# One weight load moved from ScalarE's DMA queue to GpSimd's, in front of the identity

## The chip, the cores and the metric

The kernel runs on one core of a Trainium2 chip. The metric is the device time of one execution in microseconds (us), as a median over runs. The engines are named as in the profile: PE is TensorE (matmul), PEld its weight loads, DVE VectorE, ACT ScalarE, POOL GpSimd, SP SyncE; SPq, ACTq and POOLq are the queues of instructions that these issue, DMA issues among them.

## The reference

One input x of 2048 rows and 512 columns goes through two branches that a gate mixes:

```
g = sigmoid(sum(x * gate_w, last axis))
a = attention(x): q, k, v = x @ wqkv, 32 heads of 16; row s sees the rows s, s-2, ..., s-14;
    softmax over these 8 (bfloat16), weighted sum of v, then @ wo
b = mixer(x): h = layernorm(x); u = gelu(h^T w1 + b1); y = (u w2 + b2)^T
out = g * a + (1 - g) * b
```

All inputs and the output are bfloat16. wqkv is 512 x 1536, wo 512 x 512, w1 2048 x 1792, w2 1792 x 2048.

## The kernel before, in words

The kernel is one list of operations that a planner in the same file (class `_Sched`) puts into an order for each engine. Each operation carries a duration, the buffers it reads and writes (these give waits on semaphores) and further order constraints: `order` holds operations that must be issued earlier by the plan, without a wait on their end. For the first loads the time at which they land is written by hand (`lands`). The planner walks through the operations by their ready times and the length of the work that hangs on them; then each engine runs its list in order, and no engine passes a waiting instruction of its own.

The 512 columns of x are the contraction of the projections, taken as four parts of 128 (`dt` 0 to 3). So wqkv's columns for q, k and v are each loaded as rows of 128 by part: "Wq's first quarter" is the first 128 rows of the 512 columns for q, 128 KB, one row of 1 KB for each partition. The projections need x transposed (`XT`), 512 rows of x at a time (a block `sb`, 0 to 3).

How the program begins:

- SP issues the DMA transpose of x's first 512 rows, columns 128 to 511 (line 473), then Wq's second, third and fourth quarter (one DMA each), Wk in two halves, two tiles of x, the DMA transpose of the second block (line 460), and further loads.
- ACT issues "the plain columns" (line 479): columns 0 to 127 of the first 512 rows, not transposed, 128 KB; and behind it Wq's first quarter (line 481, through `ld_w`, whose DMA appears as line 429 like that of all plain DMAs).
- POOL writes the identity (line 417), 128 x 128, and clears the padding columns of K and V (lines 420, 421) and the bias row buffer (line 517).
- PE runs five matmuls over 512 columns and one over 256 on a constant (line 536), whose result nobody reads; then four matmuls of the plain columns against the identity (line 544), which transpose them; and another constant matmul. ACT (line 553) and DVE (line 555) each evict half of the transposed columns into XT's first part. DVE's first operation is a reduction of the identity to a 0/1 matrix (line 424) that is used later for summing over heads.
- Then come PE's projections (line 617). For the first block, eight results (four column groups of q, four of k) are summed in eight PSUM banks at once: four matmuls for q's column groups with part 0, four with part 1, four with part 2, four with part 3; then k's with parts 0 and 1, and with parts 2 and 3. So the first four matmuls need Wq's first quarter and the transposed plain columns, the next four Wq's second quarter and the DMA transpose, and so on. The rest of the projections (other blocks, then v) sum four matmuls each in four banks in turn, and ACT evicts them (lines 625, 628).

What comes after: DVE multiplies q with shifted k (line 688), PE sums the products over each head (line 696, two bursts), DVE and ACT do the softmax, ACT's DMAs spread the weights over partitions, DVE forms the weighted sums of v (lines 795 to 800). Beside it DVE takes the layernorm's statistics (line 572), ACT applies it (line 596), and PE runs the mixer's two matmuls (lines 810 and 860). At the end PE multiplies by wo (line 876) and DVE adds the gated branches (line 897), and the rows go out by DMA. The order on DVE and ACT is largely written out by hand in chains of names; PE's main matmuls are in one chain with the product sums placed by the planner.

The issue order around the change is set by these lines: `first_loads` gives Wq's first quarter its queue, and one line orders it behind the plain columns.

Of the kernel before, what the change touches and what calls it, by code (L numbers as in the profile page):

```python
# [333 lines left out]
def bass_gated_mix__sliding_local_dilated__mixer_token_mlp__prompt_kernel(nc, A_x, A_wqkv, A_wo, B_x, B_w1, B_b1, B_w2, B_b2, gate_w, out, dbg=None):  # L334
    with contextlib.ExitStack() as es:
# [75 lines left out]
        def psub(ap_, p0, np_, offs, dims):  # L411
# [5 lines left out]
        c_ident = A("pool", lambda e: e.affine_select(out=IDENT, in_=nc.const_aps.tensor(1.0, [128, 128], BF16), pattern=[[1, 128]], compare_op=ALU.is_equal,  # L417
                                                     fill=0.0, base=0, channel_multiplier=-1),
                    0.4, writes=["ident"], name="ident")
# [8 lines left out]
        def mk_dma(dst, src):  # L428
            return lambda e: e.dma_start(dst, src)  # L429
# [3 lines left out]
        def throttle():  # L433
            return [init_dmas[-5]] if len(init_dmas) >= 5 else []

        def prev_dma():
            return [init_dmas[-1]] if init_dmas else []

        def ld_x(t0, n, q="sp"):
            ds = sch.dsem("x%d" % t0)  # L440
            op = sch.dma(q, mk_dma(X[:, t0:t0 + n, :], xv[:, t0:t0 + n, :]), n * 128 * D * 2, ds,
                         writes=["x%d" % t for t in range(t0, t0 + n)], deps=throttle() if q == "sp" else [], after=prev_dma() if q == "sp" else [], name="d_x%d" % t0)
            if q == "sp":
                init_dmas.append(op)
            return op

        def ld_w(tn, d0, n, q="sp"):
            ds = sch.dsem("wqkv%d_%d" % (tn, d0))
            op = sch.dma(q, mk_dma(WQKV[:, d0:d0 + n, tn * D:(tn + 1) * D], wqkv_v[:, d0:d0 + n, tn * D:(tn + 1) * D]),
                         n * 128 * D * 2, ds, writes=["wqkv%d_%d" % (tn, dt) for dt in range(d0, d0 + n)],  # L450
                         deps=throttle() if q == "sp" and n == 4 else [], after=prev_dma() if q == "sp" else [],
                         issue=0.65 if n == 4 else 0.45, name="d_wp%d_%d" % (tn, d0))
            if q == "sp":
                init_dmas.append(op)
            return op
# [14 lines left out]
        def ld_xt0():  # L470
            ds = sch.dsem("xt0")
            dst = XT[:, 1:4, 0:512]
            op = sch.dma("sp", lambda e: e.dma_start_transpose(dst, x2d[0:512, 128:512]), 512 * 384 * 2, ds, issue=1.25,
                         writes=XT0[1:4], after=prev_dma(), name="d_xt0")
            init_dmas.append(op)
            return op

        XP = view("OUTS", BF16, [(128, 4), (1, 128)])
        d_xp = sch.dma("act", mk_dma(XP, xv[:, 0:4, 0:128]), 512 * 128 * 2, sch.dsem("xp"), writes=["outs0"], issue=0.4, name="d_xp")

        first_loads = [ld_w(0, 0, 1, "act"), ld_xt0(), ld_w(0, 1, 1), ld_w(0, 2, 1), ld_w(0, 3, 1), ld_w(1, 0, 2), ld_w(1, 2, 2),
                       ld_x(0, 2)]
        ld_xt(1)
        first_loads.append(init_dmas[-1])
# [1 line left out]
            op_.lands = t_  # L486
            op_.deps.clear()
        d_xp.lands = 3.1
        first_loads[0].order.add(d_xp)
        init_dmas[:] = [first_loads[1]] + first_loads[5:]  # L490
        ld_x(2, 2)
        ld_x(4, 4)
# [558 lines left out]
```

## Time and profile before

| | us |
|---|---|
| median of 3 runs | 167.71 (167.71 to 167.93) |
| the profiled execution | 168.55 |
| its span, first to last instruction | 167.3 |
| PE busy | 162.1 |
| DVE busy | 151.3 |
| ACT busy | 75.1 |
| POOL busy | 0.7 |
| plain columns: issued by ACT, length of the issue | 0.80, 0.46 |
| Wq's first quarter: issued by ACT, length of the issue | 1.28, 0.53 |
| identity on POOL: start, length | 0.89, 0.29 |
| first projection matmul | 5.61 |

The profile is one execution; its times count from its first instruction. The issue of a DMA is an instruction on the issuing engine's queue; the data arrive later, and the DMA view of the trace gives the time from the issue's start to the landing. Matmuls overlap their neighbours, so their start distances tell their rate better than their durations. The mean clock that the profile grants PE over the span is 1.000.

### The profile page before, as it was taken

Reading aid. Unit: us, or ns where it says so; the run is one execution under the profiler, and the core shown is the slowest. Engines: PE = TensorE matmul, PEld = TensorE weight load, DVE = VectorE, ACT = ScalarE, POOL = GpSimd, SP = SyncE. Lnnn points to the kernel's source line nnn. Section 1 sums busy time; section 2 is a strip of 40 time slices with the busy share of each in tenths; the row PEclk is TensorE's granted clock in tenths of the full one; section 3 lists DMA queues with packets and bytes.
Section 4 is the critical chain, followed back from the end, with each engine's and each line's share of the span. In section 5 each row is a group of like instructions: output and inputs, shape, how many; then the busy total and the mean of one; then the engine's idle time right before and its main releaser. Section 6 shows DMA issues by size and latency. Waiting matters only on the chain.

```text
span 167.3 us, 2136 instructions
## 1 busy us (share of the span) xinstructions
PE 162.1 (97%) x845; PEld 77.5 (46%) x859; DVE 151.3 (90%) x154; ACT 75.1 (45%) x116; POOL 0.7 (0%) x8
## 2 busy tenths in 40 slices
PE   7699999999999999999999999999999999999994
PEld 2355555554454444444444444444444444444463
DVE  1055999999999999999999999999999999999896
ACT  3077688889899818793131121131231321310100
POOL 1000000000000000000000000000000000000000
PEclk9999999999999999999999999999999999999999
DMA  5999999959003846996779926462672570000454
GB/s 135 327 268 216 314 316 290 303 165 308 2 0 97 311 116 179 307 290 155 181 189 340 339 76 142 113 187 71 181 218 83 138 223 0 0 0 0 157 190 159
DMA packets 47625, 29.64 MB, mean 177 GB/s; under 512 B 9856, under 2 KB 46464, under 8 KB 47616
## 3 DMA queue, kind: packets, MB, share of 16 engines
q1 hardware_dynamic: 45120, 24.85, 54.4%
q10 hardware_dynamic: 2496, 4.66, 10.2%
q8 instruction: 7, 0.11, 0.3%
q14 instruction: 2, 0.02, 0.0%
HBM read 21.24 MB, written 2.10 MB: 140 GB/s over the span
## 4 chain that ended last, share of the span: by engine, by line
PE 91%; DMA 3%; DVE 2%; ACT 2%; issue 1%; ACTq 0%
PE ps L860 29%; PE ps L810 29%; PE ps L617 23%; PE ps L876 6%; PE ps L696 4%; DMA arena<-in_A_wqkv_dram 3%; DVE arena L897 2%; ACT L585 1%; ACT arena L628 1%; ACTq L429 0%; ACT arena L585 0%
## 5 line engine op out<-in xcount | busy, mean ns | idle before, releaser
L860 PE MATMUL ps<-arena 128*128 128x512 bf16 x220 | 48.5, 379 | 0.2
L810 PE MATMUL ps<-arena 128*128 128x512 bf16 x219 | 48.2, 379 | 0.4 <-issue 0.2
L617 PE MATMUL ps<-arena 128*128 128x512 bf16 x188 | 41.4, 379 | 1.6 <-DMA arena<-in_A_wqkv_dram 1.3
L688 DVE TENSOR_TENSOR arena<-arena 128x4096 bf16<-128x4096 bf16 (+1 forms) x12 | 35.5, 2998 | 2.5 <-ACT arena L628 2.1
L795 DVE TENSOR_TENSOR arena<-arena 128x8192 bf16<-128x8192 bf16 x8 | 35.0, 4419 | 0.0
L860 PEld LDWEIGHTS ps<-arena 128*128 128x128 bf16 x224 | 21.9, 98 | 26.4
L810 PEld LDWEIGHTS ps<-arena 128*128 128x128 bf16 x224 | 21.8, 98 | 26.6 <-ACT arena L726 0.4
L617 PEld LDWEIGHTS ps<-arena 128*128 128x128 bf16 x192 | 21.6, 113 | 21.5 <-issue 1.8
L928 ACT ACTIVATE arena<-ps,arena 128x512 bf16<-128x512 f32 x16 | 12.5, 778 | 39.4 <-PE ps L860 39.4
L798 DVE TENSOR_TENSOR arena<-arena 128x4096 bf16<-128x4096 bf16 (+1 forms) x16 | 27.0, 1751 | 0.0
L628 ACT ACTIVATE arena<-ps 128x512 bf16<-128x512 f32 x32 | 18.6, 596 | 4.5 <-PE ps L617 4.5
L831 ACT ACTIVATE arena<-ps,arena 128x512 bf16<-128x512 f32 x14 | 9.6, 687 | 22.2 <-PE ps L810 16.6
L572 DVE BATCH_NORM_STATS2 arena<-arena 128x6 f32<-128x512 bf16 x16 | 10.0, 682 | 6.1 <-DMA arena<-in_A_x_dram 6.1
L876 PE MATMUL ps<-arena 128*128 128x512 bf16 (+1 forms) x79 | 14.1, 336 | 0.1
L897 DVE SCALAR_TENSOR_TENSOR arena<-ps,arena 128x512 bf16<-128x512 f32 (+1 forms) x20 | 11.5, 637 | 0.9 <-PE ps L876 0.7
L596 ACT ACTIVATE arena<-arena 128x512 bf16<-128x512 bf16 x16 | 12.2, 804 | 0.0
L625 ACT ACTIVATE arena<-ps 128x512 bf16<-128x512 f32 x16 | 9.0, 597 | 6.2 <-PE ps L617 6.1
L876 PEld LDWEIGHTS ps<-arena 128*128 128x128 bf16 x80 | 7.8, 98 | 6.2
L672 DVE SCALAR_TENSOR_TENSOR arena<-arena 128x512 bf16<-128x512 bf16 x16 | 10.1, 689 | 0.0
L742 DVE TENSOR_TENSOR arena<-arena 128x512 bf16<-128x512 bf16 (+4 forms) x11 | 7.3, 667 | 0.6 <-ACT arena L761 0.2
L696 PE MATMUL ps<-arena 128*32 128x512 bf16 x128 | 7.3, 380 | 0.0
L726 ACT ACTIVATE arena<-ps 128x512 bf16<-128x512 f32 x8 | 4.7, 592 | 4.6 <-PE ps L696 4.6
(42 smaller groups left out, 40.0 us busy)
## 6 DMA issues: line engine op xcount, KB each, us to landing
arena<-in_B_w_dram SPq DMA_DIRECT2D x7, 1024.0 KB, 8.5
arena<-in_B_w_dram SPq DMA_DIRECT2D x8, 896.0 KB, 5.2
arena<-arena ACTq DMA_DIRECT2D x32, 128.0 KB, 2.9
arena<-in_A_x_dram SPq DMA_DIRECT2D x4, 512.0 KB, 6.1
out_dram<-arena SPq DMA_DIRECT2D x14, 128.0 KB, 1.7
arena<-in_A_x_dram SPq DMA_DIRECT2D x1, 1536.0 KB, 7.9
arena<-in_A_wqkv_dram SPq DMA_DIRECT2D x2, 256.0 KB, 3.8
arena<-in_A_x_dram SPq DMA_DIRECT2D x2, 256.0 KB, 3.6
```

Source lines behind the costliest of these rows:

```text
L596: A("act", (lambda t_: (lambda e: e.activation(out=X[:, t_, :], in_=X[:, t_, :], func=AF.Identity, scale=col(RSTD, t_), bias=col(NMR, t_)) ...
L617: ins = e.matmul(ps[:, bank, s0:s1], lhsT=lhsT, rhs=XT[:, dt, sb * 512 + s0:sb * 512 + s1], start=(dt == 0 and s0 == 0), stop=(dt == 3))
L628: return lambda e: e.activation(out=dst, in_=ps[:, bank, :], func=AF.Copy)
L688: return lambda e: e.tensor_tensor(out=PBL[buf][:, :, 512 * c0:512 * (c0 + nc_)], in0=in0, in1=in1, op=ALU.mult)
L696: ins = e.matmul(ps[32 * c:32 * c + 32, 4 + wl, :], lhsT=RP, rhs=PBL[buf][:, wl, c * 512:(c + 1) * 512], start=(dl == 0), stop=(dl == 3), ...
L795: A("dve", (lambda o_, i0, i1: (lambda e: e.tensor_tensor(out=o_, in0=i0, in1=i1, op=ALU.mult)))(pv, in0, in1), 4.4, reads=v_res + ["atx_% ...
L798: A("dve", (lambda pv_, n__: (lambda e: e.tensor_tensor(out=pv_[:, 0:n__], in0=pv_[:, 0:n__], in1=pv_[:, n__:2 * n__], op=ALU.add)))(pv, n ...
L810: ins = e.matmul(ps[:, bank, :], lhsT=W1W[:, slot, st, 128 * e_:128 * e_ + 128], rhs=X[:, st, :], start=(st == 0), stop=(st == NST - 1))
L860: ins = e.matmul(ps[:, bank, :], lhsT=W2S[slot][:, ft, 128 * e_:128 * e_ + 128], rhs=UT[:, ft, :], start=(ft == 0), stop=(ft == NFT - 1))
L876: ins = e.matmul(ps[:, bank, 0:c1 - c0], lhsT=OT[:, t, 128 * i:128 * i + 128], rhs=WO[:, t, c0:c1], start=(t == 0), stop=(t == 3))
L897: A("dve", (lambda i_, b_, c0_, c1_: (lambda e: e.scalar_tensor_tensor(out=T1[:, i_, c0_:c1_], in0=ps[:, b_, 0:c1_ - c0_], scalar=col(G, i ...
L928: A("act", (lambda i_, bank_: (lambda e: e.activation(out=T1[:, i_, :], in_=ps[:, bank_, :], func=AF.Identity, scale=col(OMG, i_), bias=co ...
```

## The change

Wq's first quarter is issued by POOL instead of ACT. The order constraint that put it behind the plain columns on ACT is gone; in its place the identity is ordered behind this issue on POOL. Size, source and destination of the transfer, the hand-written landing times and everything else stay as they are.

```
-        first_loads = [ld_w(0, 0, 1, "act"), ld_xt0(), ld_w(0, 1, 1), ld_w(0, 2, 1), ld_w(0, 3, 1), ld_w(1, 0, 2), ld_w(1, 2, 2),
+        first_loads = [ld_w(0, 0, 1, "pool"), ld_xt0(), ld_w(0, 1, 1), ld_w(0, 2, 1), ld_w(0, 3, 1), ld_w(1, 0, 2), ld_w(1, 2, 2),
...
-        first_loads[0].order.add(d_xp)
+        c_ident.order.add(first_loads[0])
```

## The prediction

> **What bounds the kernel now.** I read the page's shares of busy time and the chain that ended last first. They say which engine sets the end.
>
> ```profile
> span 167.3 us, 2136 instructions
> ...
> PE 162.1 (97%) x845; PEld 77.5 (46%) x859; DVE 151.3 (90%) x154; ACT 75.1 (45%) x116; POOL 0.7 (0%) x8
> ...
> PE 91%; DMA 3%; DVE 2%; ACT 2%; issue 1%; ACTq 0%
> ```
>
> TensorE (PE) is busy for 97% and holds 91% of the chain. The 3% of DMA is one piece. The same chain in order of time, cut to its first 14 us, shows it (start, length, what):
>
> ```profile
> 0.80 0.46 ACTq L429
> 1.25 0.03 issue
> 1.28 4.24 DMA arena<-in_A_wqkv_dram
> 5.52 0.09 issue
> 5.61 8.36 PE ps L617 x38
> ```
>
> ACT issues the plain columns of x from 0.80, then Wq's first quarter from 1.28. The quarter lands 4.24 us later, at 5.52, and the first projection matmul starts at 5.61. From there the chain is PE with pieces of ACT, down to a DVE tail. So the change touches the one transfer that sets PE's start. How much earlier PE may go is set by what else the first matmuls need. The timeline of the same stretch (start, length, engine, line) gives it:
>
> ```profile
> 0.80 1.35 SPq L473 DMA_TRANSPOSE arena<-in_A_x_dram  x1
> 0.84 2.51 PE L536 MATMUL ps<-const-bfloat16-1.0 128*128 128x512 bf16 x6 [0.84 <-PEq L1036]
> 0.89 0.29 POOL L417 TENSOR_SCALAR_AFFINE_SELECT arena<-const-bfloat16-1.0 128x128 bf16<-128x128 bf16 x1 [0.38 <-POOLq L1036]
> 3.33 0.58 PE L544 MATMUL ps<-arena 128*128 128x128 bf16 x4
> 3.71 0.63 PE L536 MATMUL ps<-const-bfloat16-1.0 128*128 128x512 bf16 x1
> 3.96 0.42 DVE L555 CAST arena<-ps 128x256 bf16<-128x256 f32 x1 [2.45 <-PE ps L544]
> ```
>
> The identity is ready at 1.18, the plain columns at 3.2, the PE transposes start at 3.33 and their second half is evicted by 4.38. So on the x side the first matmul could start near 4.43. The second group of four matmuls needs the DMA transpose and Wq's second quarter. The DMA issues that fall into 2.00 to 2.25 (size, us from the start of the issue to the landing) name both:
>
> ```profile
> arena<-in_A_wqkv_dram SPq DMA_DIRECT2D x1, 128.0 KB, 3.8
> arena<-in_A_x_dram SPq DMA_TRANSPOSE x1, 4.9
> ```
>
> The transpose, issued at 0.80, lands at 5.7. The second quarter is issued at 2.22 (SP's timeline) and lands at 2.22 + 3.8 = 6.02. That is the next wall, only half a microsecond behind the one removed.
>
> **The change, part by part.** *The quarter's issue leaves ACT.* ACT loses one issue of 0.53 us (1.28 to 1.81). ACT's table load moves up behind it. ACT's first work is the eviction at 3.74, which waits for PE: nothing gained there. The plain columns are still ACT's first issue at 0.80. SP's queue is not touched.
>
> *The quarter's issue on GpSimd (POOL).* It can start where the identity did, near 0.8. That is 0.48 earlier than 1.28. The trace of before holds no DMA that POOL issues, so both its issue time and its start are bounded by rows. The plain columns were issued at 0.80 and their queue moved 62 packets before 2.25, with none before 2.0: a start of 1.3 us. Wq's quarter was issued at 1.28, and its queue stood like this in 3.25 to 3.5:
>
> ```profile
> q1 hardware_dynamic: 272, 0.07, 122.4%
> q10 hardware_dynamic: 4, 0.00, 4.6%
> ```
>
> None of its packets ran from 3.0 to 3.25, four here: a start of 2.1 us, with the SP queue (q1) full of the transpose. From there, 3.4, to the landing at 5.52 is 2.1 us. On POOL: 0.8 + 1.3 + 2.1 = 4.2 at best, 0.8 + 2.1 + 2.1 = 5.0 with the late start. I take 4.5, nearer the first: like the plain columns it finds the DMA engines empty (no traffic before 2.0 in the DMA view). The farthest row, the slowest landing of a load in the first 14 us (a DMA transpose, 6.0), would give 6.8.
>
> *What waits behind it on POOL.* Identity, two K/V pad memsets and the bias-row memset come after the issue. An issue on ACT or SP takes 0.42 to 0.56 for plain copies here, 1.35 for the first transpose, 3.4 for a later one. The identity, 0.29, is wanted at 3.3 with the plain columns; with an issue of 0.5 it ends at 1.6, with 1.35 at 2.5. Both are hidden by the 2.1 us between 1.18 and 3.3. If it took 3.4, the identity would end at 4.5, and the eviction, 1.05 behind the transposes' start, at 5.65: slower by some 0.1. The DVE reduction over the identity goes with it and is wanted at 38.5, its engine next at 3.96. The K pad is wanted at 11.4, the bias rows at 31.4.
>
> *The shared DMA engines.* The quarter's 128 KB now run beside the plain columns instead of in the middle of the transpose. From 3 to 4 us the engines move 305 GB/s, so 128 KB cost 0.43 us of all of them. At worst the plain columns land that much later, 3.63. The evictions then end at 4.81 and the first group starts at 4.86. At best they're untouched: 4.43. I take 4.8. The transpose and the second quarter have the same bytes ahead of them as before, so I leave 5.7 and 6.02; the bounds are 0.43 earlier (the quarter runs before 2.25, when the engines still have room) and 0.1 later.
>
> *The sum.* Matmuls start 0.215 apart (5.61, 5.83, 6.04), so a group of four takes 0.86. Before: 5.61 + 0.86 = 6.47 for the second group, and its data (6.02) are there. After: the first group runs 4.8 to 5.66, the second waits for the second quarter: 6.02 + 0.09 = 6.11. Gain 6.47 - 6.11 = 0.36 us, wherever the first quarter lands before 5.16. The third and fourth quarters (issued at 2.83 and 3.29, 3.4 and 3.3 to landing) are there at 6.2 and 6.6, wanted at 6.97 and 7.83. The next x block is there at 5.27 + 5.5 = 10.8, wanted at 12.2. No further wall.
>
> *Does it reach the end?* DVE, 90% busy, could eat it. It starts its long run at 15.07 after a wait for evictions of PE's output, and near the end it waits for PE again:
>
> ```profile
> 15.07 2.29 DVE L688 TENSOR_TENSOR arena<-arena 128x4096 bf16<-128x4096 bf16 x1 [2.06 <-ACT arena L628]
> ...
> 157.35 8.29 DVE L897 SCALAR_TENSOR_TENSOR arena<-ps,arena 128x512 bf16<-128x512 f32 x15 [0.72 <-PE ps L876]
> ```
>
> Both move with PE. DVE's last load-bound work ahead of 15.07 ends at 13.02, so that wait has 2 us of room. PE's bursts over DVE's products begin at 38.5 and 61.2, 1.2 us after DVE finished them. The whole program slides by 0.36. The profiled execution took 168.55 us (span 167.3 and 1.25 around it), giving 168.19. The median of the three runs shown is 167.71, 0.84 below it; there I predict 167.35, 0.21% less. A difference under 0.2%, 0.34 us, can't be told from no change, so the forecast lies just on the faster side.
>
> **The rivals.**
> *Only the issue's lead, or less (same).* If POOL's DMA starts later than any row shows, 3.2 to 3.7 us after its issue would still land it at about 5.2 to 5.8, and the second wall stops mattering: time changes by less than 0.2%. For it: nothing in the trace shows POOL's path. Against: it needs a start over 1 us worse than the late row. [...]
>
> *POOL's DMA is late (slower).* Place: PE's wait at 5.61. It decides when the landing is behind 5.52, and shows beyond 5.86. Each microsecond behind it is a microsecond of the end: at 6.1 the time is 168.3, at the far row's 6.8 it is 169.0. For it: no row of such a DMA. Against: three rows put it at 4.2 to 5.0.
>
> *PE is still slow when it starts (slower).* The first matmuls over 512 columns average 624 ns, those from 5.61 on 379. The warm ones' weight loads stand 0.43 apart (1.22, 1.65, 2.08), the later matmuls 0.215. The change to full speed fell between 3.71, the start of the last slow one, and 5.61, with PE busy almost without a gap from 0.84 to 4.34. A plain-column landing at 3.63 opens a gap of 0.4 at 3.3. If that delayed full speed by another such stretch (3.5 us, from 0.84 to 4.34), to 7.8 or later, matmuls from 6.11 to 7.8 would run at half speed: 0.85 lost, net +0.5, 168.2, and more if later. If the change only keeps its moment, nothing is lost: half-speed matmuls from 4.86 are through with the group by 6.11 even if it falls at 5.61. [...]
>
> *More is gained (faster).* If the quarter is through early enough that the second quarter lands up to 0.43 earlier, the gain is up to 0.79: 166.92.
>
> That another order on POOL keeps the issue from being first is cheap: its memsets take 0.15 each, three of them 0.45, still under 5.16.
>
> **How the numbers follow.** The forecast's case 52%: its own range 167.15 to 167.55, by the second quarter's landing between 5.8 and 6.2; of it 44% faster by over 0.2%, 8% within. Only the lead: 9%, within. Late on POOL: 24%, of it 3% within and 21% slower; a price with no row of its own gets more than its rows would give. Slow PE: 9%, slower. More gained: 6%, faster. Sum: faster 0.50, same 0.20, slower 0.30. The range runs from 166.95, the bound of more gain, to 168.4, a landing at 6.2; left out are late landings beyond it (10%), most of the slow PE (7%) and 2% below.
>
> **What would show it.** Right: POOL's first entry is the DMA issue near 0.8, the identity ends before 3.3, the quarter lands before 5.16, the first group starts at 4.4 to 4.9, and a short wait of PE for the second quarter or the transpose ends near 6.1; the wait at 15.07 and the tail come 0.36 earlier. Wrong: PE's first wait still ends on the first quarter; the identity or the eviction at 4.38 moves beyond 5.1; matmuls of L617 average above 379 ns; or PE stands idle later on a DVE or DMA wait that before did not have.

## The result, and the profile after

The changed kernel took 170.27 us (median of four executions, 168.5 to 170.72), the kernel before 167.82 beside it (four, 167.71 to 168.03): an estimated ratio of 1.0113, with a 95% interval of 1.0075 to 1.0152. A second comparison (twelve executions of the changed kernel, 35 of the one before) gave 1.0077, interval 1.0030 to 1.0123. All ratios here leave out executions over 1.5% above the fastest of their kernel, which takes out 7 of those 35 and none of the twelve; over all of them the means are 169.83 and 168.74, a ratio of 1.0065. The change makes the kernel slower; 167.35 had been forecast.

One thing about these times has to be known before they can be read: the executions of *both* kernels lie in two groups about 2 us apart, with nothing between 169.0 and 169.7. Of 16 executions of the changed kernel, 4 lie at 168.3 to 168.5 and 12 at 169.9 to 170.7. Of 100 executions of the kernel before, timed beside the changed kernel and beside the runs below or repeated in them, 71 lie at 167.6 to 169.0 and 29 at 169.8 to 170.9. The executions shown ahead of the prediction, and those beside the first result, happened to be of the lower group.

The profiled execution of the changed kernel took 170.23. The page's lines for the span, the engines and the projections:

```profile
span 169.0 us, 2136 instructions
...
PE 163.9 (97%) x845; PEld 77.9 (46%) x859; DVE 151.3 (90%) x154; ACT 75.1 (44%) x116; POOL 1.5 (1%) x9
...
L617 PE MATMUL ps<-arena 128*128 128x512 bf16 x188 | 43.3, 391 | 1.5 <-DMA arena<-in_A_wqkv_dram 1.1
```

PE is 1.8 us busier with the same 845 matmul records, and the projections (line 617) average 391 ns instead of 379. So the time isn't in a wait: PE itself was slower. The chain of the first 14 us (start, length, what; x31 counts the matmuls that fall into these 14 us):

```profile
0.70 0.59 issue
1.29 4.08 DMA arena<-in_A_wqkv_dram
5.37 0.09 issue
5.46 8.71 PE ps L617 x31
```

The first projection starts 0.15 *earlier* than in the trace of before (5.61), and yet 31 matmuls now take longer (8.71) than 38 did (8.36). The weight loads of the same stretch show where (start, length; one load precedes each matmul):

```profile
5.43 0.14 PEld L617 LDWEIGHTS ps<-arena 128*128 128x128 bf16 x2 [1.69 <-issue]
5.84 0.15 PEld L617 LDWEIGHTS ps<-arena 128*128 128x128 bf16 x1 [0.27 <-issue]
6.27 0.15 PEld L617 LDWEIGHTS ps<-arena 128*128 128x128 bf16 x1 [0.28 <-issue]
...
8.83 0.15 PEld L617 LDWEIGHTS ps<-arena 128*128 128x128 bf16 x1 [0.28 <-issue]
9.26 4.65 PEld L617 LDWEIGHTS ps<-arena 128*128 128x128 bf16 x22 [0.28 <-issue]
```

Up to 9.26 the loads stand 0.43 apart, the pace of the constant matmuls at the start ("half pace" below); from there 22 of them take 4.65, 0.21 each ("full pace"). Nine matmuls at 0.21 extra are 1.9 us. Everything behind is only shifted: DVE's wait for the first evictions and its last wait for PE both end 1.71 later (15.07 and 157.35 before), as the span is 1.7 longer:

```profile
16.78 4.49 DVE L688 TENSOR_TENSOR arena<-arena 128x4096 bf16<-128x4096 bf16 x2 [2.33 <-ACT arena L628]
...
159.06 8.29 DVE L897 SCALAR_TENSOR_TENSOR arena<-ps,arena 128x512 bf16<-128x512 f32 x15 [0.72 <-PE ps L876]
```

And GpSimd's side, from the timeline of the start:

```profile
1.29 0.69 POOL L429 DMA_DIRECT2D arena<-in_A_wqkv_dram  x1 [0.78 <-POOLq L1036]
2.08 0.31 POOL L417 TENSOR_SCALAR_AFFINE_SELECT arena<-const-bfloat16-1.0 128x128 bf16<-128x128 bf16 x1
...
3.31 0.58 PE L544 MATMUL ps<-arena 128*128 128x128 bf16 x4
3.69 0.63 PE L536 MATMUL ps<-const-bfloat16-1.0 128*128 128x512 bf16 x1
```

The issue shows at 1.29, not near 0.8, and takes 0.69; the identity is ready at 2.39, well ahead of PE's transposes, which start when they did. PE is busy from 0.84 to 4.32, as before, and then has nothing to do until the quarter is there.

### The profile page after: what moved, and what is told of

Same layout as the page of the kernel before. It is cut to its first block, busy times and chain, and to the rows that moved or that the text cites. A ratio compares the mean times of both kernels' runs of the same rounds, so it can differ in the third digit from the quotient of the medians.

```text
span 169.0 us, 2136 instructions
## 1 busy us (share of the span) xinstructions
PE 163.9 (97%) x845; PEld 77.9 (46%) x859; DVE 151.3 (90%) x154; ACT 75.1 (44%) x116; POOL 1.5 (1%) x9
## 3 DMA queue, kind: packets, MB, share of 16 engines
q10 hardware_dynamic: 2352, 4.52, 9.9%
## 4 chain that ended last, share of the span: by engine, by line
PE 91%; DMA 2%; DVE 2%; ACT 2%; issue 1%; POOLq 0%
PE ps L860 28%; PE ps L810 28%; PE ps L617 24%; PE ps L876 6%; PE ps L696 4%; DMA arena<-in_A_wqkv_dram 2%; DVE arena L897 2%; ACT L585 1%; ACT arena L628 1%; ACT arena L585 0%; POOLq L1036 0%
## 5 line engine op out<-in xcount | busy, mean ns | idle before, releaser
L860 PE MATMUL ps<-arena 128*128 128x512 bf16 x220 | 48.5, 379 | 0.2
L810 PE MATMUL ps<-arena 128*128 128x512 bf16 x219 | 48.2, 379 | 0.4 <-issue 0.2
L617 PE MATMUL ps<-arena 128*128 128x512 bf16 x188 | 43.3, 391 | 1.5 <-DMA arena<-in_A_wqkv_dram 1.1
```

Source lines behind the costliest of these rows:

```text
L617: ins = e.matmul(ps[:, bank, s0:s1], lhsT=lhsT, rhs=XT[:, dt, sb * 512 + s0:sb * 512 + s1], start=(dt == 0 and s0 == 0), stop=(dt == 3))
L810: ins = e.matmul(ps[:, bank, :], lhsT=W1W[:, slot, st, 128 * e_:128 * e_ + 128], rhs=X[:, st, :], start=(st == 0), stop=(st == NST - 1))
L860: ins = e.matmul(ps[:, bank, :], lhsT=W2S[slot][:, ft, 128 * e_:128 * e_ + 128], rhs=UT[:, ft, :], start=(ft == 0), stop=(ft == NFT - 1))
```

## The experiments

The theory that came out of the traces, not yet shown here: PE starts at half its pace (weight loads 0.43 apart) and goes over to full pace (0.21) at a moment that is not fixed in the program; it lies ahead of 5.61 in the trace of before and at 9.26 in that of the changed kernel. If PE goes on working, this costs little. If it pauses for a microsecond behind its 3.5 us of constant matmuls (1.13 in the changed kernel's trace), the pause can push that moment to 9 or 10 us, and 7 to 11 projections run at half pace. The rivals: GpSimd's DMA, or its traffic, holds PE down; the order on GpSimd does it; the upper group is chance that has nothing to do with the first loads.

### Both kernels again, a GpSimd DMA elsewhere, and a filled pause

The first two are the kernels unchanged; then

```
late_pool (on the kernel before):
-        sch.dma("sp", mk_dma(GWB, gsrc), ...
+        sch.dma("pool", mk_dma(GWB, gsrc), ...
after_fill (on the changed kernel; four constant matmuls behind the transposes, not one):
-    w3_ = A("pe", f_warm(1), 0.43, ...
+    w3_ = A("pe", f_warm(4), 0.43, ...
```

> The kernel before once more, for a second trace of it. In the first trace PE reached full speed before its first projection matmul (5.61), and Wq's first quarter landed at 5.52. [...]

> The changed kernel once more. Its trace had nine projection matmuls 0.43 apart from 5.46 on, where the kernel before has them 0.215 apart: 9 x 0.21 = 1.9 us. [...]

> The kernel before, with a GpSimd DMA elsewhere: the broadcast of gate_w (128 KB, issued near 51 us) goes out from GpSimd instead of SP, the start is as in before. [...]

> The changed kernel with four constant matmuls instead of one behind the transposes, so that PE is busy from 0.84 to its first projection instead of stopping at 4.3. [...] Rival (the GpSimd DMA or its traffic keeps PE slow): still nine slow matmuls up to 9.3, 170.2.

| | executions | of them above 169.6 | median below 169.6 |
|---|---|---|---|
| kernel before, beside them | 35 | 10 | 168.07 |
| before, repeated | 10 | 1 | 167.94 |
| changed, repeated | 12 | 9 | 168.34 |
| GpSimd DMA at 51 us | 10 | 2 | 168.41 |
| changed, pause filled | 12 | 0 | 168.45 |

The fill removes the upper group from the changed kernel (0 of 12 against 9 of 12), with the same DMA on GpSimd: neither that DMA nor its traffic by itself holds PE down. A GpSimd DMA somewhere else doesn't raise the share (2 of 10). In the filled kernel's trace the projections have to go at half pace only to 6.67:

```profile
4.49 0.15 PEld L536 LDWEIGHTS ps<-const-bfloat16-1.0 128*128 128x128 bf16 x1 [0.28 <-issue]
5.43 0.15 PEld L617 LDWEIGHTS ps<-arena 128*128 128x128 bf16 x2 [0.79 <-issue]
...
6.67 3.35 PEld L617 LDWEIGHTS ps<-arena 128*128 128x128 bf16 x16 [0.25 <-issue]
```

The new trace of the kernel before held a second surprise. Its chain:

```profile
1.28 3.27 DMA arena<-in_A_wqkv_dram
4.55 0.09 issue
4.64 8.88 PE ps L617 x38
```

The quarter, issued by ACT at the same 1.28, landed at 4.55, not at 5.52. The one trace that the prediction worked from was not typical.

### The pause without GpSimd, the fill without GpSimd, the order on GpSimd, and the quarter first on SP

```
before_fill: the fill of after_fill, on the kernel before
pause (on the kernel before; the first four projections also wait for Wq's second quarter):
-   reads=xt_of(0, d0, d1) + ["wqkv%d_%d" % (tn, dt) for dt in range(d0, d1)],
+   reads=xt_of(0, d0, d1) + ["wqkv%d_%d" % (tn, dt) for dt in range(d0, max(d1, 2))],
ident_first (on the changed kernel):
-   c_ident.order.add(first_loads[0])
+   first_loads[0].order.add(c_ident)
sp_first_fill (on the kernel before, and f_warm(2) behind the transposes):
-   first_loads = [ld_w(0, 0, 1, "act"), ld_xt0(), ...
+   first_loads = [ld_w(0, 0, 1), ld_xt0(), ...
-   first_loads[0].order.add(d_xp)
```

> The kernel before, DMAs untouched, with four constant matmuls instead of one behind the transposes, so that PE doesn't stop before its projections. Of 45 executions of the kernel before beside the last runs, 11 were at 170.0 or more, the rest at 167.65 to 168.7. If those 11 are executions in which PE's pause before the projections cost it the full clock: none at 170 any more, all at 167.6 to 169.0. If the slow ones come from something else (DMA, chance on the chip): a quarter of them stays at 170 or more.

> The kernel before, DMAs untouched and no DMA on GpSimd; PE's first four projection matmuls also wait for Wq's second quarter, which lands at 5.5 to 6.0. So PE's pause behind the constant matmuls (from 4.3) is 1.2 us or longer in each execution, as in the changed kernel, where the quarter landed at 5.37 to 5.41 in all three traces. Theory of the pause: two groups, about 168.5 and 170.5, with most of the executions (about three in four, as in the changed kernel) in the slow one. Rival (GpSimd's DMA itself makes the slow ones frequent): a quarter slow as in before, the rest at 168.3 to 168.9.

> The changed kernel with the identity ahead of the DMA on GpSimd again; the DMA stays on GpSimd. The trace of the changed kernel shows the DMA's issue at 1.29 although GpSimd had nothing to do from 0.5, and a landing 4.1 behind the issue. If the order on GpSimd matters, the landing moves by the identity's 0.3 to 5.7 and the time by that; I expect less, issue at 1.3 to 1.6, landing at 5.4 to 5.7, the same two groups within 0.3 of 168.4 and 170.4.

> Wq's first quarter as SP's first DMA ahead of the transpose, nothing on GpSimd, and two constant matmuls instead of one behind the transposes. The step of the prediction that the quarter lands early and the second quarter is the next wall, without GpSimd's path: the quarter lands at 3 to 4, the transpose and the second quarter at 5.2 to 6.0, the second group starts at 5.6 to 6.1, no execution at 170, all at 167.4 to 168.2. Rival: the transpose, issued half a microsecond later, lands that much later and takes the gain back, 168.0 to 168.7.

| | executions | above 169.6 | median below 169.6 | ratio to before |
|---|---|---|---|---|
| kernel before, beside them | 35 | 14 | 168.34 | |
| before, pause filled | 12 | 0 | 168.64 | 1.0000 (0.9973 to 1.0027) |
| forced pause | 12 | 5 | 168.72 | 1.0024 (0.9975 to 1.0074) |
| identity first | 10 | 7 | 168.36 | 1.0081 (1.0033 to 1.0128) |
| quarter first on SP | 12 | 3 | 169.07 | 1.0026 (0.9983 to 1.0070) |

The fill removes the upper group from the kernel before as well: its 29 in 100 are the same thing. In its trace the constant matmuls end at 5.0, in that of the changed kernel at 5.5, which holds back executions whose quarter lands early: the fastest takes 168.25, beside 167.64. So the median stays (168.64 beside 168.57), while the mean of all executions falls from 169.09 to 168.61. The order on GpSimd doesn't matter: the DMA's issue moves from 1.29 to 1.38, the landing is at 5.3. The forced pause gave 5 of 12, fewer than the three in four that I expected and close to the 14 of 35 beside it.

The quarter first on SP shows what an early quarter costs its neighbours, though it isn't the predicted change without GpSimd: it also puts SP's own transpose and the second quarter later. The quarter landed at 0.80 + 2.5 = 3.3; but the plain columns, beside it, landed at 0.80 + 3.1 = 3.9 instead of 3.2, later than the prediction's bound of 3.63 for two such loads side by side, and the second quarter, issued a microsecond later behind the transpose, at 3.24 + 3.0 = 6.2:

```profile
arena<-in_A_x_dram ACTq DMA_DIRECT2D x1, 128.0 KB, 3.1
arena<-in_A_wqkv_dram SPq DMA_DIRECT2D x1, 128.0 KB, 2.5
```

PE idles 0.73 ahead of its transposes, and its trace has half-pace projections to 7.4. The executions are no two groups but spread from 168.4 to 170.5, with a median of 169.13 above both expected ranges: this early quarter is paid for elsewhere.

### The pause again, with and without GpSimd's DMA, a shorter fill, and GpSimd's DMA alone

```
pause_again: pause once more
pause_pool (on pause): before the identity GpSimd loads a second copy of the quarter into ATT,
  + c_ident.order.add(sch.dma("pool", mk_dma(<ATT, first 512 columns>, wqkv_v[:, 0, 0:D]), ...))
before_fill2 (on the kernel before): f_warm(2) for f_warm(1) behind the transposes
pool_alone (on late_pool): + byname["d_xa"].deps.add(byname["d_gw"])
```

> The kernel with the forced pause once more (5 of its 12 executions were at 170.4 or more, 7 at 168.6 to 169.4; of the executions with the quarter on GpSimd, in either order there, 19 of 26 were slow). Theory of the pause alone: the share rises towards three in four, 8 to 10 of 12 slow. Rival (GpSimd's early DMA adds something): 3 to 6 of 12 again.

> The forced pause, Wq's first quarter still on ACT, and beside it a second copy of the same quarter that GpSimd loads as its first instruction, ahead of the identity, into a buffer nobody reads before it is overwritten. This adds 128 KB to the first loads, so 0.3 to 0.5 on all executions against the forced pause: groups near 169.1 and 171.0. Theory of the pause alone: the same share of slow executions as with the forced pause in this batch. [...]

> The kernel before with two constant matmuls instead of one behind the transposes. PE is then busy to 4.8, and four of them, which end near 5.3, held back the first projections in executions in which the quarter lands at 4.6. Two shouldn't: the fast ones at 167.6 to 168.6 as before, and fewer slow ones than in before, 0 to 2 of 12, since the pause is 0.4 shorter. If only the landing counts: 3 to 5 of 12 slow.

> The price of a GpSimd DMA by itself: the broadcast of gate_w (128 KB) issued by GpSimd near 51 us, with SP's next load (1.5 MB of x) held back until it has landed. In the run without that wait its first packet ran 4.3 behind its issue and it landed 6.2 behind, with SP's load in front of it; at the kernel's start, beside the transpose, 2.55 and 4.1. If traffic of the other queues holds it: 2.0 to 3.0 to the landing. If the path has a fixed price: 3.5 to 4.1 again. The same load from SP in the kernel before took 3.9, with the 1.5 MB behind it.

| | executions | above 169.6 | median below 169.6 |
|---|---|---|---|
| kernel before, beside them | 16 | 4 | 168.19 |
| forced pause, again | 6 | 5 | 168.62 (one) |
| forced pause and GpSimd DMA | 6 | 5 | 169.26 (one) |
| before, shorter fill | 12 | 3 | 168.27 |

With the pause forced and no DMA on GpSimd, 10 of 18 executions in all are in the upper group; with an early DMA on GpSimd 12 of 16, 7 of 10 and 5 of 6. So the upper group needs no DMA on GpSimd. Neither whether forcing the pause raises its share over the kernel before's (10 of 18 against 18 of the 51 beside), nor whether GpSimd's early DMA raises it further (24 of 32 against 10 of 18), is settled by these numbers. The shorter fill neither helps nor harms (ratio 0.9999, interval 0.9980 to 1.0019), with 3 of 12 in the upper group where I expected at most 2: it shortens the pause by 0.4 only, and a late quarter still leaves one (0.63 in its trace).

The two forced-pause kernels are one program, and their traces, of 169.34 and 170.78, show the two cases. First the one of 169.34, then the one of 170.78:

```profile
6.36 3.60 PEld L617 LDWEIGHTS ps<-arena 128*128 128x128 bf16 x18 [2.61 <-issue]
```

```profile
5.71 0.14 PEld L617 LDWEIGHTS ps<-arena 128*128 128x128 bf16 x2 [1.99 <-issue]
...
9.54 0.15 PEld L617 LDWEIGHTS ps<-arena 128*128 128x128 bf16 x1 [0.28 <-issue]
9.91 0.55 PEld L617 LDWEIGHTS ps<-arena 128*128 128x128 bf16 x3 [0.22 <-issue]
```

The second started its projections 0.65 earlier and still ended later, because ten matmuls ran at half pace. PE's work up to 4.3 is the same in both. In the second the first quarter had landed early, 3.3 behind its issue at 1.28, and PE was waiting for the second: it isn't the quarter's landing that makes PE slow.

GpSimd's DMA with no other traffic beside it, 128 KB as the quarter is, with its time to the landing, and the plain columns that ACT issues at the start of the same kernel:

```profile
arena<-in_gate_w_dram POOLq DMA_DIRECT2D x1, 128.0 KB, 3.5
```

```profile
arena<-in_A_x_dram ACTq DMA_DIRECT2D x1, 128.0 KB, 2.4
```

Both are issued while the DMA engines are empty; GpSimd's takes 1.1 us more, though the two differ in shape (rows of 1 KB against pieces of 256 bytes). At the kernel's start the quarter took 4.1 on GpSimd in both traces of the changed kernel, 0.6 more than this load alone.

### Which executions of the kernel before are slow

Six more traces of the kernel before, unchanged.

> A further trace of the kernel before, unchanged (first of four). In eight traces with the quarter on ACT it landed 3.3 behind its issue three times (4.55) and 3.9 to 4.4 behind it five times (5.2 to 5.7); none of the kernel before's own traces fell on a slow execution. Theory of the pause: an execution near 170 has the quarter's landing at 5.1 or later, a pause of 0.8 or more, and 9 to 11 projection matmuls 0.43 apart; an execution with the landing at 4.6 is never near 170, whatever its matmuls' first spacing. Rival (slow executions come without regard to the landing): a slow one with a landing at 4.6 is as likely as any.

> Second of the four further traces of the kernel before; expected as for the first: near 170 only with the landing at 5.1 or later.

> Third of the four further traces of the kernel before; expected as for the first: near 170 only with the landing at 5.1 or later.

> Fourth of the four further traces of the kernel before; expected as for the first: near 170 only with the landing at 5.1 or later. One execution in three or four of this kernel is near 170, so that one or two of the four should show it.

> The kernel before once more, for a trace of an execution near 170, which the four looks didn't catch. They gave landing and time 4.53: 167.65, 4.55: 168.02, 5.54: 168.67, 5.72: 168.75. Theory of the pause: a landing near 4.55 gives 167.6 to 168.2, a landing from 5.1 on 168.3 to 168.8 or, with slow matmuls, 170 or more. Rival: 170 or more with a landing near 4.55.

> As for the look before it: near 4.55 gives 167.6 to 168.2, from 5.1 on 168.3 to 168.8 or 170 and more; the rival, 170 or more with a landing near 4.55.

With the first two traces that makes eight, here in order of the quarter's landing:

| landing | first projection | time |
|---|---|---|
| 4.44 | 4.54 | 168.24 |
| 4.53 | 4.62 | 167.65 |
| 4.55 | 4.64 | 168.02 |
| 4.55 | 4.64 | 168.19 |
| 5.52 | 5.61 | 168.55 |
| 5.54 | 5.63 | 168.67 |
| 5.72 | 5.81 | 168.75 |
| 5.75 | 5.84 | 170.33 |

The landing comes in two kinds too, 4.4 to 4.6 and 5.5 to 5.8, and no execution of these with the early one is above 168.3. The one near 170 has the latest landing and seven half-pace intervals, not the nine to eleven that I expected, from 5.81 to 8.79:

```profile
5.81 0.14 PEld L617 LDWEIGHTS ps<-arena 128*128 128x128 bf16 x2 [2.11 <-issue]
6.22 0.15 PEld L617 LDWEIGHTS ps<-arena 128*128 128x128 bf16 x1 [0.27 <-issue]
...
8.79 2.31 PEld L617 LDWEIGHTS ps<-arena 128*128 128x128 bf16 x11 [0.28 <-issue]
```

In the execution with the landing at 4.44 the projections also began at half pace, but PE had paused for only 0.33 and went over at 6.15:

```profile
4.50 0.14 PEld L617 LDWEIGHTS ps<-arena 128*128 128x128 bf16 x2 [0.89 <-DVE arena L555]
...
5.77 0.15 PEld L617 LDWEIGHTS ps<-arena 128*128 128x128 bf16 x1 [0.28 <-issue]
6.15 4.86 PEld L617 LDWEIGHTS ps<-arena 128*128 128x128 bf16 x23 [0.23 <-issue]
```

In the trace of 168.19, with the landing at 4.55, half pace lasted to 5.81 after a pause of 0.31. So half pace isn't made by the pause; what differs with the pause is how long it lasts: to 8.79 here, behind one of 1.56.

Two things in the kept traces close the account. The first is that nothing else differs. In 13 traces, whatever their edit, the time behind the start of ACT's first eviction of projections is the same, 159.9 to 160.0; before and after:

```profile
8.62 2.06 ACT L625 ACTIVATE arena<-ps 128x512 bf16<-128x512 f32 x4 [4.49 <-PE ps L617]
10.32 2.06 ACT L625 ACTIVATE arena<-ps 128x512 bf16<-128x512 f32 x4 [6.22 <-PE ps L617]
```

The second is the clock itself. The traces of before and after hold the stretch of full TensorE clock with its start and length. In the changed kernel it starts where the loads change their spacing, at 9.26, and lasts 160.43 us; in the kernel before it starts at 4.48, ahead of the projections, and lasts 163.84. Both stretches reach past the last instruction, at 169.0 and 167.3: full pace, once there, stayed to the end. In 19 traces the spacing of the loads tells the moment. In the five above 170 it is 8.79 to 10.10, and PE had idled 1.13 to 1.56 us ahead of its first projection. In four others whose projections began at half pace it is 5.45 to 6.67; the idle time ahead of them is 0.31 and 0.33 in two of the four, and none shows in the filled one. One more, the quarter first on SP, changes at 7.4, after the 0.73 that PE idled there ahead of its transposes. Nine traces have their projections at full pace from the first on, and among these are pauses as long: 1.26 in the first trace of before, 2.05 in the forced pause of 169.34.

With the fills (0 of 24 executions in the upper group with four constant matmuls, on either kernel) this makes the pause the cause, though not every long pause has the effect; what decides between the two cases isn't shown. The fill also makes the constant work longer; but in the early landings above the constant work was as short as in the upper group, and full pace came by 6.15.

## Why the prediction was wrong, point by point

- *What bounds the kernel, and the slide to the end*: right. PE's start is on the chain, and what happened there reached the end undiminished (1.71 at DVE's first and last wait).
- *The landing of 5.52 as the thing to beat*: this step failed first. It is one of two kinds. In half of the kernel before's traces the quarter lands near 4.5, so that the first projection starts near 4.6, and PE waits for the landing by 0.3 to 0.5 only. The 0.84 by which the profiled execution lay over the median was carried along as an offset; but the three runs behind the median, at 167.71 to 167.93, lie where the early landings do (167.65 to 168.24). So the gain of 0.36 was taken off a time that most likely held it already. One execution of the kernel before shows the predicted case as a whole, with the quarter at 4.53, four projections at full pace and a wait below 0.1 for the next load, and took 167.65:

```profile
4.58 0.58 PEld L617 LDWEIGHTS ps<-arena 128*128 128x128 bf16 x4 [0.90 <-DVE arena L555]
5.53 5.54 PEld L617 LDWEIGHTS ps<-arena 128*128 128x128 bf16 x27 [0.37 <-issue]
```

- *GpSimd's issue and landing*: "near 0.8", and 4.5 between 4.2 and 5.0. Measured: 1.29, and 5.37 to 5.41 in the two traces of the changed kernel, outside the bounds. Both terms were off: the issue shows 0.5 later than I took it, and from there 4.1 went by instead of 3.7. Rows of ACT's queue were no bound for GpSimd's DMA, which took 3.5 even alone, beside ACT's 2.4. So the change replaces a landing that is early in half of the traces by one that was late in each of its own: the lower group's median is 168.34 (three executions) beside 168.07, 0.3 us. With the identity first it was 168.36 beside 168.34, so this part is small and not sure.
- *The second wall*: the second quarter landed at 2.23 + 3.4 = 5.6 in the changed kernel and the transpose at 0.81 + 4.5 = 5.3. With the first quarter at 5.37 and its four matmuls behind it, neither was a limit. Nothing of the 0.36 could come that way; even at full pace the second group would have started at 5.46 + 0.86 = 6.32, 0.15 earlier than in the trace of before.
- *POOL's other instructions*: right. The identity, 1.2 later, cost nothing.
- *Matmuls 0.215 apart from the first projection on*: this term of the sum failed with the larger price. Nine or more stood 0.43 apart, 1.9 us.
- *The rival of PE being still slow*: this is what happened, at over twice the price of its mildest case (0.85 lost was forecast, 1.9 measured), but it got 9%, and its place was wrong. I looked for a gap at 3.3, ahead of the transposes; the plain columns didn't move at all (2.4 to the landing as before). The pause that matters stood in the profile shown: 1.26 us of PE between 4.34 and 5.61. I read full pace behind it as a property of the program. It was luck: the full clock had come at 4.48 there, and the same program paused and went on at half pace in another execution.
- *The rival of a late landing on GpSimd*: decided, as stated, from 5.52 on; it landed just ahead of that.
- *The rival of only the issue's lead, or less*: 9%, and right on the landing, which it put at 5.2 to 5.8. Its sum doesn't come out: a start 3.2 to 3.7 behind the issue at 0.8 and the 2.1 from start to landing that the forecast uses make 6.1 to 6.6.

The sum by groups: 9 of 12 instead of 10 of 35 in the upper group, which lies 1.95 higher in the changed kernel, are (0.75 - 0.29) x 1.95 = 0.9 us; the lower group, 0.3 higher, adds 0.2 for the 25 of 35. Together they are the 1.1 between the means, 169.83 and 168.74.

What stays open is what sets the moment of full pace. No run varies it by itself, and it differs widely: with the pause filled in both kernels, full pace came by 4.42 in one trace (the weight load there takes 0.10, not 0.15) and at 6.67 in the other. Why the quarter on ACT lands in two ways, and whether GpSimd's early DMA moves the moment of full pace, stays open too.

## What to carry to other kernels

Where a kernel warms PE up with constant matmuls, try whether it gains when they reach to the first real matmul: a pause of a little over a microsecond between the two (1.13 to 1.56 in the traces) cost about 2 us here, in a share of the executions (9 of 12 of the changed kernel, 29 of 100 of the one before), and the profile you look at may be one of the lucky ones. Before a prediction rests on one transfer's landing, compare the profiled execution with the median; if it lies some tenths of a per cent off, the transfer that you want to move may be what differs. A small load that is wanted first gained nothing from GpSimd's queue here, although it had no other load ahead of it there (landing at 5.37 to 5.41, on ACT at 4.44 to 5.75); and moved to the head of SP's queue it delayed what it passed (the plain columns landed at 3.9 instead of 3.2).

## What the runs showed of the hardware

- GpSimd's DMA of 128 KB took 3.5 us from issue to landing with nothing beside it, 3.9 to 4.5 at the kernel's start and 6.2 beside SP's load of 1.5 MB (issued at 51.00, none of its packets ran before 55); ACT's, issued into empty DMA engines, took 2.4. Its issue took 0.69 on GpSimd, and it moved the quarter in 48 packets where ACT's queue counts 144 fewer of its own (2496 to 2352 on q10).
- One program's first quarter lands in one of two ways, about 1 us apart (4.4 to 4.6 or 5.5 to 5.8), with the issue at 1.28 in all eight traces.
- The clock row of the page says nothing of the half pace. It is 9 in all slices in the changed kernel's execution with nine half-pace projections and in that of before with none, and the mean stands at 1.0 for all 20 profiled executions. The spacing of the weight loads shows the pace (0.43 and 0.21 apart).
- The full clock came at a place that differs between executions of one program: in the eight traces of the kernel before, ahead of the first projections in four, and at 5.45, 5.81, 6.15 and 8.79 in the others.
